# Gate products of a gated MLP read their weight sums where VectorE forms them, and ring loads and row reads take another order

## The chip, the cores and the metric

The kernel runs on one core of one Trainium2 chip. The metric is the device time of one execution, in microseconds (us). A profiled execution also leaves a trace of every instruction and every DMA.

## The reference, cut to what matters

Sigmoid attention over 8 batches, 12 heads, 448 tokens and 64 values a head, and behind it a gated MLP with a spatial product between tokens:

```python
scores = scale * np.matmul(q, k.transpose(0, 1, 3, 2)) - np.log(S)
attn = 1.0 / (1.0 + np.exp(-scores))
x = np.matmul(attn, v)            # heads side by side: (8, 448, 768)
h = np.maximum(x @ w_in, 0.0)     # (8, 448, 1024)
u, v = h[..., :512], h[..., 512:]
v_n = (v - mean(v)) / np.sqrt(var(v) + 1e-06)
v_s = np.einsum('ts,bsd->btd', w_spatial, v_n) + b_spatial[None, :, None]
out = (u * v_s) @ w_out           # (8, 448, 768)
```

## The kernel before, in words

The work goes in four rounds of two batches (`m` 0 to 3; the text counts rounds 1 to 4, so `m == BY_BLOCKS` is round 3). A round is attention, then the gate products (x with the v half of w_in, called w_g), the up products (x with w_u), the spatial products, and the output products (w_out). Every operand is split into a high and a low float32r part, and a product is three products of parts.

In rounds 3 and 4 the gate, up and output products go by blocks: each weight matrix is cut into 2 by 2 blocks, called 11, 12, 21 and 22, and seven products of block sums (a scheme of Strassen's kind, with the sums s1 to s4 in place of plain block 21 and others) take the place of eight. `by_blocks` runs over the seven, in a fixed order: ORDER_U is 11, 12, s2, s3, s1, s4, 22, ORDER_1 is 11, 12, s3, s2, s1, s4, 22. Each of the seven is two results (i = 0, 1) of nine products, so one stage is 14 slots of nine. After every slot `then(mv, i)` copies or adds the result (mv names the moving operand: 11, 21, t2, t3, t1, 22, t4). Products that share a bank of PSUM wait for the copy before them.

A block and its low part take 768 KB. A ring in SBUF (`block`, `load_block`) holds four blocks, HELD, of the seven; the rest are loaded as room comes free. The blocks lie in DRAM, where `weight_sums` put the sums: VectorE adds and subtracts, ScalarE casts the high part, VectorE forms the low part, and SP writes both out. For w_g this happens in the attention of round 3, in `spare` steps. There the plain w_g lies in SBUF too (`w_g_2`), and `keep_gate_blocks` writes its blocks to DRAM. After attention, round 3 loads the ring of w_g from DRAM again, and then that of w_u. The tags w_u, w_g and w_out are regions of SBUF used in turn by several tiles: the tile `whole`, in which attention leaves unsplit results, lies in w_out's, and `us`, the up results, in w_g's.

The gate results come with columns over partitions, but the normalization needs rows. `by_tokens` turns them: `turn` transposes quarters on VectorE and writes them to DRAM with four DMAs each (`vt` to `v`, L890), and `load` reads rows back (`rv`, L906) in four reads: a (tiles 4, 5), b (6), c (0, 1), d (2, 3). Tiles 4 to 6 need the second batch's quarters only. `steps` then takes each through `relu`, `moments` (statistics on VectorE, 1/std on GpSimd, mean subtracted on ScalarE) and `scaled` (ScalarE and VectorE), one step for each call of `spare(1)`, which `ungated` makes after every slot of the up stage. All engines run in the program's order (`in_program_order`), SP's DMA queue too: a DMA that waits holds those behind it. The tiles vt and rv share the tag tmp with three buffers.

Before, SP's order around the up stage is: the last `turn`'s writes, four blocks of w_out, the reads a and b in the second slot, then w_u's fifth block, the read c, and so on.

Of the kernel before, what the change touches and what calls it, by code (L numbers as in the profile page):

```python
# [14 lines left out]
P = 128  # L15
# [20 lines left out]
def attn_gmlp_kernel(  # L36
# [65 lines left out]
    def gate_weights(name):  # L102
        w = gate_region(name)[:, : NCC * 2 * F]
        return w.rearrange("p (k a f) -> p k a f", k=NCC, a=2)
# [378 lines left out]
    NAMES = ("11", "12", "21", "22")  # L483
    HELD = 4
# [22 lines left out]
    def gate_block(name):  # L507
        m, k = NAMES.index(name) // 2, NAMES.index(name) % 2
        return w_g[-1][:, k * KH : (k + 1) * KH, :, m * 2 * P : (m + 1) * 2 * P].bitcast(F32)

    def keep_gate_blocks():
        w7, order = KINDS["g"]
        for name in NAMES:
            if name in order:
                by = w7[order.index(name)].rearrange("p a (k c) -> p a k c", k=KH)
                for a in range(2):
                    nc.sync.dma_start(by[:, a], gate_block(name)[:, :, a])
# [7 lines left out]
    def weight_sums(stage, kind):  # L525

        w7, order = KINDS[kind]

        def whole(t):
            return t.rearrange("p (k c) -> p k c", k=KH) if kind == "g" else t  # L530

        def low(i):
            return stage[:, i, 1]

        def high(i):
            return stage[:, i, 0].bitcast(F32R)

        def add(i, a, b, op=ALU.add):
            nc.vector.tensor_tensor(whole(low(i)), a, b, op=op)

        def part(name, a):
            return gate_block(name)[:, :, a] if kind == "g" else plain(w_u[0], name, a)

        def finish(i, name):
            nc.vector.tensor_sub(low(i).bitcast(F32R), low(i), high(i).bitcast(F32))
            nc.sync.dma_start(w7[order.index(name)], stage[:, i])

        def cast(i):
            nc.scalar.copy(high(i), low(i))

        add(0, part("21", 0), part("21", 1))
        yield True
        add(0, whole(low(0)), part("22", 0))
        yield True
        add(0, whole(low(0)), part("22", 1))
        yield True
        cast(0)
        add(1, whole(low(0)), part("11", 0), ALU.subtract)
        yield True
        add(1, whole(low(1)), part("11", 1), ALU.subtract)  # L560
        yield True
        finish(0, "s1")
        yield True
        cast(1)
        add(2, part("11", 0), part("21", 0), ALU.subtract)
        yield True
        add(2, whole(low(2)), part("11", 1))
        yield True
        add(2, whole(low(2)), part("21", 1), ALU.subtract)
        yield True  # L570
        cast(2)
        add(3, part("12", 0), whole(low(1)), ALU.subtract)
        yield True
        finish(1, "s2")
        yield True
        add(3, whole(low(3)), part("12", 1))
        yield True
        cast(3)
        finish(2, "s3")
        yield True  # L580
        finish(3, "s4")
        yield True
# [108 lines left out]
    def values_by_blocks(m):  # L691
# [82 lines left out]
        turn, steps = by_tokens(m)  # L774

        def then(mv, i):
# [18 lines left out]
            elif mv == "22":  # L795
                turn(1, 0, px[i], i)
            elif mv == "t4":
                nc.vector.tensor_add(r2[:, i], py[i], r2[:, i])
                if i:
                    turn(0, 1, r2)  # L800

        def stationary(w, i, k):
            return w[:, :, (k * 2 + i) * P : (k * 2 + i + 1) * P]

        by_blocks(m, "g", stationary, x, KH, {X: px, W: pw, Y: py}, then, ORDER_1)
# [68 lines left out]
    def by_tokens(m):  # L874
# [26 lines left out]
        def load(ts):  # L901
            rv = work.tile([P, 2, 512], F32, tag="tmp", name=f"rv_{m}_{ts[0]}", bufs=3)
# [47 lines left out]
        def steps():  # L950
            a, b, c, d = (4, 5), (6,), (0, 1), (2, 3)
            yield True
            load(a)
            load(b)
            yield True
# [6 lines left out]
            load(d)  # L962
            scaled(a)
            moments(b)
            yield True
            relu(c)
            scaled(b)
# [4 lines left out]
            scaled(c)  # L972
            moments(d)
# [4 lines left out]
        return turn, steps  # L978
# [91 lines left out]
    def by_blocks(m, kind, stationary, moving, nk, ps, then, order):  # L1070
# [3 lines left out]
        for pos, name in enumerate(order):  # L1074
            mv, to = OPERANDS[name]
            if not whole:
# [19 lines left out]
            if not whole and pos + HELD < NB:  # L1096
# [4 lines left out]
    def gated_by_blocks(m):  # L1101
# [176 lines left out]
        if m >= BY_BLOCKS:  # L1278

            def ungated(mv, i):  # L1280
# [13 lines left out]
                spare(1)  # L1294

            by_blocks(m, "u", stationary, x, KH, {X: px, W: pw, Y: py}, ungated, ORDER_U)
# [374 lines left out]
    for m in range(B // 2):  # L1671
        if m == 1:
            stage = const.tile([P, 4, 2, BLOCK], F32, tag="w_out", name="w_u_sums")
            jobs.append(weight_sums(stage, "u"))
            w_g.append(gate_weights("w_g_2"))
            late[8] = [lambda: nc.sync.dma_start(w_g[-1].bitcast(F32), w_g_kept)]
        ring = []
        if m >= BY_BLOCKS:
            whole_x["tile"] = const.tile([P, 4, KH, S], F32, tag="w_out", name=f"whole_{m}")
            if m == BY_BLOCKS:  # L1680
                stage = const.tile([P, 4, 2, BLOCK], F32, tag="w_u", name="w_g_sums")
                jobs.append(weight_sums(stage, "g"))
# [9 lines left out]

            if m > BY_BLOCKS:
                late[8].append(lambda: gate_ring(range(HELD)))
# [6 lines left out]
        if m in (1, BY_BLOCKS):  # L1701
            w_u.append(const.tile([P, 2, NCC * F], F32R, tag="w_u", name=f"w_u_{m}"))
        if m == BY_BLOCKS:
            gate_ring(range(HELD))
        if m:
# [7 lines left out]
        if m >= BY_BLOCKS:  # L1713
            values_by_blocks(m)
            w_out.append(const.tile([P, 2, NFC * DM], F32R, tag="w_out", name=f"w_out_{m}"))
            for pos in range(HELD):
                load_block("out", ORDER_1, pos)
# [91 lines left out]
```

## Time and profile before

| what | value |
| --- | --- |
| time, median of 3 runs | 684.9 us (684.85 to 686.63) |
| the profiled execution, its own time | 684.99 us |
| its span, first to last instruction | 683.2 us |
| TensorE busy, share of the span | 638.3 us, 93% |
| VectorE busy | 468.1 us, 69% |
| ScalarE busy | 336.6 us, 49% |
| mean granted TensorE clock | 0.968 of full speed |

PE is TensorE's products, PEld its weight loads, DVE VectorE, ACT ScalarE, POOL GpSimd, SP the engine that issues most DMAs. A busy share is an average over stages; a stage's own limit is read from what ended its waits. L with a number is a line of the kernel before.

### The profile page before, as it was taken

To read this page: it belongs to the slowest core of one execution; us is meant where nothing else is said; L and a number is where in the kernel's file an instruction comes from. 1 tells how busy PE (TensorE), PEld (TensorE's weight loads), DVE (VectorE), ACT (ScalarE), POOL (GpSimd) and SP (SyncE) were. 2 spreads that over 40 slices of the span, in tenths; PEclk is the share of its full clock that TensorE was granted. 3 is DMA by queue.
4 is the path that set the end of the run, shared out by engine and by line. 5 is a ranking of instruction groups with operands and counts; after the bars stand their busy time and mean duration, and the time that the engine had idled before them with its cause. 6 is when DMAs were issued, how large, how long until landed. Compare 5 with 4: busy or idle time off the path is not lost.

```text
span 683.2 us, 10332 instructions
## 1 busy us (share of the span) xinstructions
PE 638.3 (93%) x4136; PEld 495.2 (72%) x4136; DVE 468.1 (69%) x645; ACT 336.6 (49%) x437; POOL 21.5 (3%) x63
## 2 busy tenths in 40 slices
PE   9999999999999999999999799359999999954997
PEld 3655889997566789998666599259975568944997
DVE  4989789897697968396986852345775558425373
ACT  6986313254788363252888520441457765035033
POOL 0000020000000020000000000100000000011000
PEclk9999999999999999999999899879999999985999
DMA  8756433499347840447394789501583385771035
GB/s 294 263 166 216 123 122 96 172 333 316 133 138 286 336 172 1 138 166 270 140 320 176 300 288 270 234 16 68 180 307 114 114 366 131 179 305 62 0 115 185
DMA packets 52815, 130.03 MB, mean 190 GB/s; under 512 B 18720, under 2 KB 27680, under 8 KB 52640
## 3 DMA queue, kind: packets, MB, share of 16 engines
q1 hardware_dynamic: 52336, 129.04, 53.9%
q8 instruction: 32, 0.52, 0.3%
q10 hardware_dynamic: 432, 0.34, 0.2%
q14 instruction: 15, 0.12, 0.0%
HBM read 95.03 MB, written 34.34 MB: 189 GB/s over the span
## 4 chain that ended last, share of the span: by engine, by line
PE 72%; DVE 14%; DMA 5%; ACT 5%; issue 2%; SPq 1%; POOL 0%; ACTq 0%; DVEq 0%
PE pav L1509 13%; PE psc L372 12%; PE o L1086 11%; PE pg L1022 7%; PE ux L1086 6%; PE pv L454 5%; PE vx L1086 5%; PE pav L421 5%; DMA rv<-v 3%; PE uy L1086 3%; PE psc L354 2%; PE vy L1086 2%; DVE wval_s L154 1%; ACT rv L910 1%; DVE stats L917 1%
## 5 line engine op out<-in xcount | busy, mean ns | idle before, releaser
L336 ACT ACTIVATE ats<-psc,bias_s 128x896 f32<-128x896 f32 x102 | 95.2, 1008 | 19.4 <-PE pav L1509 13.3
L372 PE MATMUL psc<-qks 64*128 64x448 f32 x840 | 88.7, 364 | 1.4 <-ACT at L336 1.4
L372 PEld LDWEIGHTS psc<-qks 64*128 64x128 f32 x840 | 77.2, 184 | 16.9 <-issue 6.3
L1509 PE MATMUL pav<-ats,v 64*64 64x448 f32 x720 | 76.0, 539 | 0.0
L1086 PE MATMUL ux<-x_s,w_u 128*128 128x448 f32 x162 | 44.0, 435 | 34.0 <-ACT us L1288 18.7
L1086 PEld LDWEIGHTS ux<-x_s,w_u 128*128 128x128 f32 x162 | 37.2, 234 | 40.3 <-ACT us L1288 19.7
L1022 PE MATMUL pg<-w_sp_s,mlp 128*128 128x448 f32 x320 | 65.8, 363 | 0.0
L1022 PEld LDWEIGHTS pg<-w_sp_s,mlp 128*128 128x128 f32 x320 | 59.7, 188 | 5.3 <-issue 1.2
L1509 PEld LDWEIGHTS pav<-ats,v 64*64 64x64 f32 x720 | 28.2, 132 | 37.5 <-issue 25.8
L1086 PE MATMUL o<-x_s,w_out 128*128 128x448 f32 x270 | 55.0, 362 | 0.0
L1086 PEld LDWEIGHTS o<-x_s,w_out 128*128 128x128 f32 x270 | 50.6, 188 | 3.4
L322 DVE TENSOR_TENSOR qks<-raw,qks 128x848 fp32r<-128x848 f32 x46 | 47.4, 1038 | 1.1 <-ACT qks L315 0.2
L1086 PE MATMUL vx<-x_s,w_g 128*128 128x448 f32 x144 | 32.5, 384 | 4.3 <-DMA w_g<-w_g 3.9
L1086 PEld LDWEIGHTS vx<-x_s,w_g 128*128 128x128 f32 x144 | 28.6, 201 | 8.6 <-issue 5.4
L1509 PE MATMUL pav<-at,v 64*64 64x448 f32 x216 | 32.0, 536 | 0.0
L1155 ACT CAST x_s<-g 128x896 fp32r<-128x896 f32 (+1 forms) x11 | 9.6, 876 | 39.6 <-DVE g L1152 37.5
L454 PE MATMUL pu<-x_s,w_u_s 128*128 128x448 f32 x144 | 29.0, 362 | 0.0
L454 PE MATMUL pv<-w_g_s,x_s 128*128 128x512 f32 x126 | 28.9, 390 | 0.0
L454 PE MATMUL pv<-w_g,x_s 128*128 128x512 f32 x126 | 28.9, 390 | 0.0
L454 PEld LDWEIGHTS pu<-x_s,w_u_s 128*128 128x128 f32 x144 | 27.0, 188 | 1.8
L336 ACT ACTIVATE at<-psc,bias_s 128x896 f32<-128x896 f32 x18 | 18.1, 1010 | 20.7 <-PE psc L354 14.7
L454 PEld LDWEIGHTS pv<-w_g_s,x_s 128*128 128x128 f32 x126 | 23.6, 188 | 5.6 <-PE pav L421 0.7
(234 smaller groups left out, 1057.4 us busy)
## 6 DMA issues: line engine op xcount, KB each, us to landing
raw<-qk_dram SPq DMA_DIRECT2D x47, 456.0 KB, 5.6
w_u<-w_u SPq DMA_DIRECT2D x21, 768.0 KB, 11.0
w_out<-w_out SPq DMA_DIRECT2D x21, 768.0 KB, 6.4
v<-v_dram SPq DMA_DIRECT2D x24, 448.0 KB, 4.2
w_g<-w_g SPq DMA_DIRECT2D x14, 768.0 KB, 7.3
wraw<-w_in_dram SPq DMA_DIRECT2D x12, 512.0 KB, 4.5
v<-vt SPq DMA_DIRECT2D x32, 112.0 KB, 2.5
w_g_kept<-w_g_s SPq DMA_DIRECT2D x6, 512.0 KB, 5.4
```

The source lines that it names most:

```text
L154: nc.vector.scalar_tensor_tensor(l, low, 29, l, op0=ALU.logical_shift_right, op1=ALU.bitwise_or)
L322: nc.vector.tensor_sub(s[:, 1], loaded[b, hp][:, HALF:], s[:, 0].bitcast(F32))
L336: nc.scalar.activation(at, src, AF.Sigmoid, bias=bias_s, scale=QK)
L354: nc.tensor.matmul(psc[odd * HALF : (odd + 1) * HALF, j, :S], raw[rows, :HALF], raw[rows, HALF + Q :], start=True, stop=True,)
L372: nc.tensor.matmul(psc[:, j, :S], st[rows, k : k + P], mv[rows, Q:PART], start=i == 0, stop=i == len(ops) - 1,)
L421: nc.tensor.matmul(pav[heads, odd, :S], vt[rows, t, heads], at[rows, j], start=start, stop=t == NFULL,)
L454: nc.tensor.matmul(ps, st, mv, start=i == 0, stop=i == len(ops) - 1)
L910: nc.scalar.activation(rv, rv, AF.Relu)
L1022: nc.tensor.matmul(pg[:, i, :S], st, mv, start=n == 0 and not ended, stop=n == len(ops) - 1 and ended,)
L1086: nc.tensor.matmul(out_ps, stationary(w, i, k)[:, a], moving[mv][k][c], start=(to, i) not in started and n == 0, stop=n == len(ops) - 1, s ...
L1155: nc.scalar.copy(homes[name][0][:, i], src[:, i])
L1509: ins = nc.tensor.matmul(pavs[pair][heads, i % 2, :S], vt[rows, t if t == NFULL else t + i % 2 * (NFULL + 1), heads], at[rows, j], start=i ...
```

## The change

In round 3 the gate products read plain blocks out of w_g as it lies, and the sums out of the blocks in which VectorE forms them. These are the four blocks of w_u's ring, so that the tile of w_u is made before attention, and w_u's first four blocks are loaded one by one as the gate products are through with the sums. The unsplit sums lie in the tile `whole`. In round 4 w_u's first four blocks are loaded in attention's first and second group. In rounds 3 and 4 the first four blocks of w_out are loaded from the up stage's last four sums on, not ahead of the stage; the reads a and b are issued before the last quarter is turned, b goes to `wval_s` instead of a buffer of the tag tmp, and the steps stand in another order over the slots, d's read after a's scaling. The copy of w_g for rounds 2 and 3 lies GAP elements further on in its region.

```diff
@@ -99,8 +99,8 @@
     def gate_region(name, dtype=F32R):
         return const.tile([P, NCC * 2 * F + NEAR], dtype, tag="w_g", name=name)
 
-    def gate_weights(name):
-        w = gate_region(name)[:, : NCC * 2 * F]
+    def gate_weights(name, at=0):
+        w = gate_region(name)[:, at : at + NCC * 2 * F]
         return w.rearrange("p (k a f) -> p k a f", k=NCC, a=2)
 
     w_g = [gate_weights("w_g_s")]
@@ -481,6 +481,7 @@
     ORDER_1 = ("11", "12", "s3", "s2", "s1", "s4", "22")
     ORDER_OUT = ("11", "s2", "s3", "s1", "s4", "22", "12")
     NAMES = ("11", "12", "21", "22")
+    SUMS_G = tuple(name for name in ORDER_1 if name not in NAMES)
     HELD = 4
     w7_u, w7_out, w7_g = (
         dram.tile([NB, P, 2, BLOCK], F32, name=f"w7_{n}") for n in ("u", "out", "g")
@@ -506,7 +507,7 @@
 
     def gate_block(name):
         m, k = NAMES.index(name) // 2, NAMES.index(name) % 2
-        return w_g[-1][:, k * KH : (k + 1) * KH, :, m * 2 * P : (m + 1) * 2 * P].bitcast(F32)
+        return w_g[-1][:, k * KH : (k + 1) * KH, :, m * 2 * P : (m + 1) * 2 * P]
 
     def keep_gate_blocks():
         w7, order = KINDS["g"]
@@ -514,7 +515,7 @@
             if name in order:
                 by = w7[order.index(name)].rearrange("p a (k c) -> p a k c", k=KH)
                 for a in range(2):
-                    nc.sync.dma_start(by[:, a], gate_block(name)[:, :, a])
+                    nc.sync.dma_start(by[:, a], gate_block(name)[:, :, a].bitcast(F32))
 
     def keep_plain(w7, order, w):
         for name in NAMES:
@@ -522,58 +523,55 @@
                 at = NAMES.index(name) * BLOCK
                 nc.sync.dma_start(w7[order.index(name)], w[:, :, at : at + BLOCK].bitcast(F32))
 
-    def weight_sums(stage, kind):
+    def weight_sums(kind, stage, sum_at):
 
         w7, order = KINDS[kind]
 
         def whole(t):
             return t.rearrange("p (k c) -> p k c", k=KH) if kind == "g" else t
 
-        def low(i):
-            return stage[:, i, 1]
-
         def high(i):
-            return stage[:, i, 0].bitcast(F32R)
+            return stage(i)[:, 0]
 
         def add(i, a, b, op=ALU.add):
-            nc.vector.tensor_tensor(whole(low(i)), a, b, op=op)
+            nc.vector.tensor_tensor(whole(sum_at(i)), a, b, op=op)
 
         def part(name, a):
-            return gate_block(name)[:, :, a] if kind == "g" else plain(w_u[0], name, a)
+            return gate_block(name)[:, :, a].bitcast(F32) if kind == "g" else plain(w_u[0], name, a)
 
         def finish(i, name):
-            nc.vector.tensor_sub(low(i).bitcast(F32R), low(i), high(i).bitcast(F32))
-            nc.sync.dma_start(w7[order.index(name)], stage[:, i])
+            nc.vector.tensor_sub(stage(i)[:, 1], sum_at(i), high(i).bitcast(F32))
+            nc.sync.dma_start(w7[order.index(name)], stage(i).bitcast(F32))
 
         def cast(i):
-            nc.scalar.copy(high(i), low(i))
+            nc.scalar.copy(high(i), sum_at(i))
 
         add(0, part("21", 0), part("21", 1))
         yield True
-        add(0, whole(low(0)), part("22", 0))
+        add(0, whole(sum_at(0)), part("22", 0))
         yield True
-        add(0, whole(low(0)), part("22", 1))
+        add(0, whole(sum_at(0)), part("22", 1))
         yield True
         cast(0)
-        add(1, whole(low(0)), part("11", 0), ALU.subtract)
+        add(1, whole(sum_at(0)), part("11", 0), ALU.subtract)
         yield True
-        add(1, whole(low(1)), part("11", 1), ALU.subtract)
+        add(1, whole(sum_at(1)), part("11", 1), ALU.subtract)
         yield True
         finish(0, "s1")
         yield True
         cast(1)
         add(2, part("11", 0), part("21", 0), ALU.subtract)
         yield True
-        add(2, whole(low(2)), part("11", 1))
+        add(2, whole(sum_at(2)), part("11", 1))
         yield True
-        add(2, whole(low(2)), part("21", 1), ALU.subtract)
+        add(2, whole(sum_at(2)), part("21", 1), ALU.subtract)
         yield True
         cast(2)
-        add(3, part("12", 0), whole(low(1)), ALU.subtract)
+        add(3, part("12", 0), whole(sum_at(1)), ALU.subtract)
         yield True
         finish(1, "s2")
         yield True
-        add(3, whole(low(3)), part("12", 1))
+        add(3, whole(sum_at(3)), part("12", 1))
         yield True
         cast(3)
         finish(2, "s3")
@@ -771,7 +769,7 @@
             "p (i s) -> p i s", i=2
         )
         sums["r"] = r1, r2, r3
-        turn, steps = by_tokens(m)
+        turn, first_loads, steps = by_tokens(m)
 
         def then(mv, i):
             if mv == "11":
@@ -798,11 +796,22 @@
                 nc.vector.tensor_add(r2[:, i], py[i], r2[:, i])
                 if i:
                     turn(0, 1, r2)
+                else:
+                    first_loads()
+
+        def source(name):
+            if m > BY_BLOCKS:
+                w = block("g", ORDER_1.index(name))
+            elif name in SUMS_G:
+                w = block("u", SUMS_G.index(name))
+            else:
+                return gate_block(name).rearrange("p k a c -> p a k c")
+            return w.rearrange("p a (k c) -> p a k c", k=KH)
 
         def stationary(w, i, k):
-            return w[:, :, (k * 2 + i) * P : (k * 2 + i + 1) * P]
-
-        by_blocks(m, "g", stationary, x, KH, {X: px, W: pw, Y: py}, then, ORDER_1)
+            return w[:, :, k, i * P : (i + 1) * P]
+
+        by_blocks(m, "g", stationary, x, KH, {X: px, W: pw, Y: py}, then, ORDER_1, source)
         jobs.append(steps())
 
     def gate_values(m, ts):
@@ -899,7 +908,10 @@
         state = {}
 
         def load(ts):
-            rv = work.tile([P, 2, 512], F32, tag="tmp", name=f"rv_{m}_{ts[0]}", bufs=3)
+            if len(ts) > 1:
+                rv = work.tile([P, 2, 512], F32, tag="tmp", name=f"rv_{m}_{ts[0]}", bufs=3)
+            else:
+                rv = wval_s[:, :1024].bitcast(F32).rearrange("p (i f) -> p i f", i=2)
             state[ts] = [rv]
             at = ts[0] * P
             src = rows[at : at + len(ts) * P].rearrange("(t p) f -> p t f", p=P)
@@ -947,11 +959,13 @@
                     )
                 vns[t] = vn
 
-        def steps():
-            a, b, c, d = (4, 5), (6,), (0, 1), (2, 3)
-            yield True
+        a, b, c, d = (4, 5), (6,), (0, 1), (2, 3)
+
+        def first_loads():
             load(a)
             load(b)
+
+        def steps():
             yield True
             relu(a)
             yield True
@@ -959,23 +973,26 @@
             moments(a)
             relu(b)
             yield True
-            load(d)
             scaled(a)
             moments(b)
             yield True
+            load(d)
+            scaled(b)
+            yield True
+            yield True
             relu(c)
-            scaled(b)
             yield True
             moments(c)
             relu(d)
             yield True
             scaled(c)
+            yield True
             moments(d)
             yield True
             scaled(d)
             yield True
 
-        return turn, steps
+        return turn, first_loads, steps
 
     def cols_of(b):
         return slice(0, S) if b % 2 else slice(512 - S, 512)
@@ -1067,13 +1084,15 @@
         "s1": ("t1", X), "s4": ("22", X), "22": ("t4", Y),
     }
 
-    def by_blocks(m, kind, stationary, moving, nk, ps, then, order):
+    def by_blocks(m, kind, stationary, moving, nk, ps, then, order, source=None):
 
         started = set()
         whole = kind == "out" and not m
         for pos, name in enumerate(order):
             mv, to = OPERANDS[name]
-            if not whole:
+            if source:
+                w = source(name)
+            elif not whole:
                 w = block(kind, pos)
             elif name in NAMES:
                 at = NAMES.index(name) * BLOCK
@@ -1093,7 +1112,10 @@
                     )
                 started.add((to, i))
                 then(mv, i)
-            if not whole and pos + HELD < NB:
+            if kind == "g" and m == BY_BLOCKS:
+                if name in SUMS_G:
+                    load_block("u", ORDER_U, SUMS_G.index(name))
+            elif not whole and pos + HELD < NB:
                 load_block(kind, order, pos + HELD)
 
     hid = {}
@@ -1292,7 +1314,10 @@
                 elif mv == "t4":
                     nc.vector.tensor_add(r2[:, i], py[i], r2[:, i])
                 spare(1)
-
+                if i and mv in after:
+                    load_block("out", ORDER_1, after.index(mv))
+
+            after = [OPERANDS[name][0] for name in ORDER_U[-HELD:]]
             by_blocks(m, "u", stationary, x, KH, {X: px, W: pw, Y: py}, ungated, ORDER_U)
             spare(99)
             for fcs in (lo_fc, hi_fc):
@@ -1671,15 +1696,24 @@
     for m in range(B // 2):
         if m == 1:
             stage = const.tile([P, 4, 2, BLOCK], F32, tag="w_out", name="w_u_sums")
-            jobs.append(weight_sums(stage, "u"))
-            w_g.append(gate_weights("w_g_2"))
+            jobs.append(
+                weight_sums("u", lambda i: stage[:, i].bitcast(F32R), lambda i: stage[:, i, 1])
+            )
+            w_g.append(gate_weights("w_g_2", GAP))
             late[8] = [lambda: nc.sync.dma_start(w_g[-1].bitcast(F32), w_g_kept)]
         ring = []
         if m >= BY_BLOCKS:
             whole_x["tile"] = const.tile([P, 4, KH, S], F32, tag="w_out", name=f"whole_{m}")
             if m == BY_BLOCKS:
-                stage = const.tile([P, 4, 2, BLOCK], F32, tag="w_u", name="w_g_sums")
-                jobs.append(weight_sums(stage, "g"))
+                w_u.append(const.tile([P, 2, NCC * F], F32R, tag="w_u", name=f"w_u_{m}"))
+                sum_rooms = [whole_x["tile"][:, n].rearrange("p k s -> p (k s)") for n in (0, 1, 0, 3)]
+                jobs.append(
+                    weight_sums(
+                        "g",
+                        lambda i: block("u", SUMS_G.index(f"s{i + 1}")),
+                        lambda i: sum_rooms[i][:, :BLOCK],
+                    )
+                )
                 late[4] = [keep_gate_blocks]
             late[8] = [lambda: jobs.append(wholes(m))]
 
@@ -1690,7 +1724,13 @@
                 for pos in ps:
                     load_block("g", ORDER_1, pos)
 
+            def up_ring(ps):
+                for pos in ps:
+                    load_block("u", ORDER_U, pos)
+
             if m > BY_BLOCKS:
+                late[0] = [lambda: up_ring(range(2))]
+                late[4] = [lambda: up_ring(range(2, HELD))]
                 late[8].append(lambda: gate_ring(range(HELD)))
         attention(m)
         slots_of_mlp(m)
@@ -1698,11 +1738,8 @@
         more = m < B // 2 - 1
         if m:
             spare(99)
-        if m in (1, BY_BLOCKS):
+        if m == 1:
             w_u.append(const.tile([P, 2, NCC * F], F32R, tag="w_u", name=f"w_u_{m}"))
-        if m == BY_BLOCKS:
-            gate_ring(range(HELD))
-        if m:
             for pos in range(HELD):
                 load_block("u", ORDER_U, pos)
         if m == 1:
@@ -1713,8 +1750,6 @@
         if m >= BY_BLOCKS:
             values_by_blocks(m)
             w_out.append(const.tile([P, 2, NFC * DM], F32R, tag="w_out", name=f"w_out_{m}"))
-            for pos in range(HELD):
-                load_block("out", ORDER_1, pos)
         else:
             for ts in ((0, 1), (2, 3), (4, 5), (6,)):
                 gate_values(m, ts)
```

## Rows read from the trace of the kernel before

**Rows 1.** Windows: time, then busy time by engine, granted clock, DMA share, GB/s.
```profile
381.30:412.80 31.50, 27.56 (x129) 25.59 (x127) 20.89 (x25) 9.32 (x15) 0.00 (x0) 0.89 0.90 318
412.80:460.10 47.30, 29.57 (x128) 26.18 (x127) 16.85 (x33) 17.14 (x27) 3.59 (x8) 0.82 0.48 171
...
562.60:588.80 26.20, 25.84 (x130) 23.55 (x127) 19.08 (x23) 9.33 (x15) 0.00 (x0) 1.00 0.53 135
588.80:637.00 48.20, 31.90 (x129) 27.93 (x128) 16.85 (x33) 17.14 (x27) 3.59 (x8) 0.79 0.48 167
...
385.30:388.90 3.60, 3.59 (x10) 3.21 (x11) 3.57 (x5) 0.99 (x2) 0.00 (x0) 0.50 1.02 427
...
423.60:427.40 3.80, 3.80 (x20) 3.24 (x18) 0.00 (x0) 0.00 (x0) 0.00 (x0) 1.00 1.00 411
```

**Rows 2.** Timeline of TensorE, round 3: start, duration, instructions, idle before and releaser.
```profile
385.31 9.71 PE L1086 MATMUL vx<-x_s,w_g 128*128 128x448 f32 x36 [3.94 <-DMA w_g<-w_g]
...
434.39 3.73 PE L1086 MATMUL ux<-x_s,w_u 128*128 128x448 f32 x9 [6.97 <-ACT us L1286]
...
450.97 5.76 PE L1086 MATMUL ux<-x_s,w_u 128*128 128x448 f32 x18 [10.18 <-ACT us L1288]
...
477.39 10.97 PE L1086 MATMUL o<-x_s,w_out 128*128 128x448 f32 x54
```

**Rows 3.** Timeline of TensorE, gate and up stages of round 4.
```profile
568.94 2.08 PE L1086 MATMUL vx<-x_s,w_g 128*128 128x448 f32 x9 [0.30 <-ACT vr L778]
...
588.85 3.76 PE L1086 MATMUL ux<-x_s,w_u 128*128 128x448 f32 x18
592.45 3.76 PE L1086 MATMUL uy<-x_s,w_u 128*128 128x448 f32 x18
...
610.60 3.73 PE L1086 MATMUL ux<-x_s,w_u 128*128 128x448 f32 x9 [7.18 <-ACT us L1286]
...
627.18 6.35 PE L1086 MATMUL ux<-x_s,w_u 128*128 128x448 f32 x18 [8.53 <-ACT us L1288]
```

**Rows 4.** Timeline of ScalarE in the up stage of round 3.
```profile
428.98 1.06 ACT L910 ACTIVATE rv<-rv 128x1024 f32<-128x1024 f32 x1 [11.79 <-DMA rv<-v]
...
432.07 1.33 ACT L925 ACTIVATE rv<-rv,mean 128x512 f32<-128x512 f32 x2 [2.03 <-DVE mean L923]
...
433.83 0.51 ACT L1286 COPY us<-ux 128x448 f32<-128x448 f32 x1
...
437.51 0.72 ACT L925 ACTIVATE rv<-rv,mean 128x512 f32<-128x512 f32 x1 [1.94 <-DVE mean L923]
...
444.16 1.04 ACT L910 ACTIVATE rv<-rv 128x1024 f32<-128x1024 f32 x1
...
450.40 0.51 ACT L1288 COPY us<-ux 128x448 f32<-128x448 f32 x1
```

**Rows 5.** Timeline of SP's DMA queue around the up stage of round 3.
```profile
410.25 2.43 SPq L890 DMA_DIRECT2D v<-vt  x4
...
416.89 2.33 SPq L501 DMA_DIRECT2D w_out<-w_out  x4
419.26 0.95 SPq L906 DMA_DIRECT2D rv<-v  x2
...
436.44 0.37 SPq L906 DMA_DIRECT2D rv<-v  x1
```

**Rows 6.** DMA issues, median us to landing: 405 to 440, last row 436 to 437.
```profile
rv<-v SPq DMA_DIRECT2D x3, 512.0 KB, 9.7
v<-vt SPq DMA_DIRECT2D x12, 112.0 KB, 2.5
...
rv<-v SPq DMA_DIRECT2D x1, 512.0 KB, 3.6
```

**Rows 7.** Timeline of VectorE at attention's end, rounds 3 and 4.
```profile
382.97 1.08 DVE L730 TENSOR_TENSOR whole<-pav,whole 128x896 f32<-128x896 f32 x1
...
562.74 1.09 DVE L730 TENSOR_TENSOR whole<-pav,whole 128x896 f32<-128x896 f32 x1
```

## The prediction

> **What bounds the kernel now.** I read the page first (TensorE is busy for most of the span, so only its gaps can pay), then TensorE's timeline for its idle, then the stages of rounds 3 and 4 as windows, then the timelines of ScalarE and of SP's DMA queue to see what ends those gaps. In the page's slices TensorE is at its lowest in two places, and both are the up products (the u stage) of a round that goes by blocks. Attention has no gap worth naming. The gate stage (g) of round 3 takes 31.5 us, the same 126 products in round 4 take 26.2; the u stages take 47.3 and 48.2 [rows 1]. Nine products take 1.80 us when nothing waits (592.45 − 588.85 for 18) [rows 3], so 14 such slots are 25.2 us, and the u stages lose 22.1 and 23.0 us. Slots count from T, the stage's start (412.86 in round 3, 588.85 in round 4).
>
> In g of round 3 the reader sees 3.94 us for a DMA of w_g's ring, and behind it 36 products in 9.71 us instead of 7.2 [rows 2]. In both u stages the two large idles, 6.97 and 10.18 us in round 3 [rows 2], 7.18 and 8.53 in round 4 [rows 3], end with a ScalarE copy out of a bank that the next products write. The copy is not slow: it stands in ScalarE's order behind a step on the rows of v. The first of these steps, relu(a), starts at 428.98, 16.1 us after T, after 11.79 us of waiting for rv's DMA, and from there to the copy at 450.40 ScalarE and VectorE hand the rows to and fro without a pause [rows 4]. That read is late because SP issued it at 419.26, directly behind four w_out blocks of 768 KB issued from 416.89, which nobody needs before 477.39 [rows 2, 5]; it took 9.7 us to land, where a later read of the same size with nothing ahead took 3.6 [rows 6]. So what ends last in u is the row chain, and it starts late.
>
> **The change, part by part.**
>
> *w_g as it lies and its sums in place.* Removes seven ring loads of round 3 and the 3.94 us wait. Its products then start with the end of attention, as in round 4 (26.2). But VectorE is later here: the first full sum of the last pair (L730) starts at 382.97, 1.6 us after attention's end at 381.4, in round 4 0.1 us after 562.6 [rows 7], and ScalarE's copies, which already cost round 4 0.30 us [rows 3], stand behind it. So 26.2 + 1.5 = 27.7: gain 3.8 us, bounds 3.0 (a further 0.8) to 5.3 (as round 4). The sums keep their VectorE and ScalarE instructions, with other addresses: nothing. That products read w_g in a longer stride I take at nothing, since 128 columns still lie together; a loss is bounded in the rivals.
>
> *The ring loads of w_u.* Round 3: each is issued when a sum's block is free, the first four blocks of 3.6 us before T; a block of 768 KB takes 1.9 us at 411 GB/s [rows 1], so they land in time. Round 4: they move from the end of attention, behind w_g's, into attention's first two groups, behind loads of q and k, where SP next waits for TensorE anyway; nothing, at worst 3.8 us twice (two blocks ahead of a needed load).
>
> *w_out's loads and the first reads.* In SP's order the reads a and b now stand ahead of the last four transposed writes, and the w_out blocks behind the read d. For read a: the four writes before it are issued from 410.25 to 412.68, T − 0.2 [rows 5], and land 2.5 us after issue [rows 6], at T + 2; issue 0.5 and landing 3.6 [rows 6] give relu(a) at A = T + 5 to 6. In round 3 w_u blocks stand on both sides of those writes; 1.9 us of their 3.8 lie in the way, less what overlaps: A = T + 6.5. In round 4 there are none, but VectorE's first statistic stands behind its sum for the third slot (ends near T + 6.2, and it comes 1.1 us after relu(a) starts), which acts like A = T + 5.1. Read b needs no third buffer now (it goes to wval_s, last read in attention), and read d waits for scaled(a), as before.
>
> *The new order of steps.* What TensorE meets is the copy of the first t1 sum, which the products of "22" wait for at T + 18.0 (ten slots). Ahead of it on ScalarE, from relu(a): to the end of b's mean, 428.98 to 438.23, less the 0.41 of a copy that moves, 8.84; two copies and the scaling of b, 0.41 + 0.72 + 0.41 = 1.54; relu(c) and moments(c), as a's from 428.98 to 433.40, 4.42; relu(d) 1.04 [rows 4]; the copy until its products run, 450.40 to 450.97, 0.57 [rows 2, 4]. Sum 16.4, so the stage loses D = A + 16.4 − 18.0 = A − 1.6. That is 4.9 us in round 3 and 3.5 in round 4, nearly all in one idle before "22". An idle of 3.94 us was followed by half clock (9.71 for 7.2, and 0.50 granted) [rows 1, 2], one of 0.30 was not (2.08 for nine) [rows 3]. 3.5 is nearer 3.94, so I take a fall in both rounds at 2.2 us each, between 9.71 − 7.2 = 2.5 and 3.73 − 1.80 = 1.9 [rows 2]; bounds 0 and 2.5. Scaled(d) ends within T + 25 + D, when the spatial products begin with other tiles: nothing. Read c is needed at A + 10.4 and can be issued from T + 7.5, after the last writes land; read d at A + 14.8, and its buffer is free at A + 7.5 (436.44 against 428.98) [rows 4, 5]: both in time. Block "22" of w_u stands behind d on SP, issued near T + 13, needed at T + 21.6 + D; with 3.6 us as for a read: in time. The w_out blocks follow it; the first is needed 17 us after the stage's end.
>
> Sum: 3.8 + (22.1 − 4.9 − 2.2) + (23.0 − 3.5 − 2.2) = 3.8 + 15.0 + 17.3 = 36.1 us. The profiled execution took 684.99 us, of which 683.20 are span; the median of the runs is 684.9. 685.0 − 36.1 = 648.9.
>
> **The rivals.**
>
> *The reads land late all the same.* If writes and w_u's blocks in the queue keep relu(a) until T + 10 to 13 (the 9.7 us landing [rows 6] in place of 3.6 gives T + 12), D is 8.4 to 11.4, and the sum 3.8 + 45.1 − 4.4 − 2D = 27.7 to 21.7: 657 to 663. For it: a read waits for DRAM writes whose landing was covered by w_out's issue before, so its price is seen nowhere. Against: the writes' own 2.5 us [rows 6], and 3 MB less ahead of the read. The Trainium skill speaks for it (DMA: Bandwidth & Descriptors, "Anatomy of one DMA — SWDGE (gpsimd) path"): the semaphore comes only once the last byte is confirmed in its target, DRAM being the heaviest. Its fixed cost is some 2 us, with which the row of 2.5 agrees. Chance 0.17.
>
> *All goes well.* A at the floor in both rounds and no fall of the clock: 3.8 + 18.6 + 19.5 = 41.9, so 643. Against it: the idle of 3.5 us left. Chance 0.13.
>
> *Slower.* SP takes its queue in order, and now reads that wait stand ahead of writes and of w_u's blocks 5 to 7. If they hold SP, relu(a) and the blocks are late together, and TensorE pays 1 us for each. It decides from 2(A − 1.6) = 45.1 + 3.8, A = T + 26, 10 us later than now. Nothing in the rows holds a read so long. Slower 0.03, and 0.03 for stopping near there, at no change.
>
> **How the numbers follow.** Forecast 0.64, its own range 645 to 655: upward A two us later in both rounds (+4) and the smaller gain in g, downward one clock fall less and g as in round 4 (−2.2, −1.5). I say 649. The range 642 to 660 leaves out the two ends at or above the old time (0.06), the late half of the first rival (0.07) and some of the second (0.02). A difference of 0.3% is about what a measurement of this kernel can tell from none. Faster 0.94, same 0.03, slower 0.03.
>
> **What would show it.** The g stage of round 3 without a DMA wait, 27 to 28 us. On SP, the reads directly behind "22"'s four writes and w_out after the read d. Relu(a) at T + 5 to 7 instead of 16. One idle of 3 to 5 us before "22" and little before t1; u stages of 30 to 33 us. No new idle in attention. I am wrong if relu(a) comes after T + 8, if the chain from it to the t1 copy isn't near 16 us, or if attention of rounds 3 and 4 grows.

## The result, and the profile after

The changed kernel takes 651.4 us (median of 4 runs, 649.57 to 653.22), the kernel before 685.24 beside it: a ratio of 0.9503, 95% interval 0.9466 to 0.9539. The forecast was 649 in 642 to 660. The profiled execution took 649.57 us with a span of 647.2, against 684.99 and 683.2. It is the fastest of the four (649.57, 649.99, 652.82 and 653.22), so what is read from its trace, 36.0 us of span, is 2 us more than the 33.8 between the medians.

The windows of the two gate and up stages after, with the columns of [rows 1]:

```profile
382.00:409.80 27.80, 25.90 (x131) 23.59 (x128) 20.72 (x25) 9.33 (x15) 0.00 (x0) 1.00 0.42 102
409.80:442.50 32.70, 27.60 (x127) 24.73 (x126) 14.31 (x30) 15.54 (x25) 3.60 (x8) 0.95 0.87 298
545.50:571.70 26.20, 25.84 (x130) 23.55 (x127) 19.06 (x23) 9.33 (x15) 0.00 (x0) 1.00 0.53 134
571.70:600.90 29.20, 25.83 (x128) 23.53 (x128) 14.37 (x30) 15.59 (x25) 3.59 (x8) 1.00 0.79 276
```

Against [rows 1] the gate stage of round 3 went from 31.5 to 27.8 us, the up stages from 47.3 and 48.2 to 32.7 and 29.2. Of the 37.3 us that these three stages gave, 27.6 are idle of TensorE. The other 9.7 are busy time: it fell from 27.56, 29.57 and 31.90 us to 25.90, 27.60 and 25.83 for about the same products, as the granted clock of the stages rose from 0.89, 0.82 and 0.79 to 1.00, 0.95 and 1.00. TensorE's timeline after shows what idle is left, round 3 first, round 4 last:

```profile
387.50 2.08 PE L1105 MATMUL vx<-x_s,w_g 128*128 128x448 f32 x9 [1.60 <-ACT vr L776]
...
428.46 5.46 PE L1105 MATMUL ux<-x_s,w_u 128*128 128x448 f32 x18 [3.65 <-ACT us L1308]
435.20 3.88 PE L1105 MATMUL ux<-x_s,w_u 128*128 128x448 f32 x18 [1.27 <-ACT us L1310]
...
586.81 3.87 PE L1105 MATMUL ux<-x_s,w_u 128*128 128x448 f32 x18 [0.51 <-ACT us L1308]
593.55 3.88 PE L1105 MATMUL ux<-x_s,w_u 128*128 128x448 f32 x18 [2.86 <-ACT us L1310]
```

The DMA wait of 3.94 us is gone, a wait of 1.60 for ScalarE's copies stands in its place, and idles of 6.97 to 10.18 [rows 2, 3] became 0.51 to 3.65. L1308 copies the t2 sums, for which the t1 products wait, and L1310 the t1 sums, for which the products of "22" wait. ScalarE's timeline tells why, with T now 409.80 and 571.74:

```profile
419.15 1.06 ACT L922 ACTIVATE rv<-rv 128x1024 f32<-128x1024 f32 x1 [5.03 <-DMA rv<-v]
...
433.69 1.04 ACT L922 ACTIVATE rv<-rv 128x1024 f32<-128x1024 f32 x1
434.64 0.51 ACT L1310 COPY us<-ux 128x448 f32<-128x448 f32 x1
...
577.50 1.06 ACT L922 ACTIVATE rv<-rv 128x1024 f32<-128x1024 f32 x1 [1.43 <-DMA rv<-v]
```

Relu(a) starts at T + 9.35 in round 3 and T + 5.76 in round 4, before at T + 16.1 [rows 4]. From there to the copy of the first t1 sum it is 15.5 us (434.64 − 419.15) instead of 21.4. SP's queue in round 3 has the reads ahead of the last quarter's writes, and w_out last:

```profile
407.76 2.46 SPq L899 DMA_DIRECT2D v<-vt  x4
410.31 1.65 SPq L502 DMA_DIRECT2D w_u<-w_u  x1
414.96 0.38 SPq L918 DMA_DIRECT2D rv<-v  x1
...
415.94 2.26 SPq L899 DMA_DIRECT2D v<-vt  x4
...
427.13 2.13 SPq L502 DMA_DIRECT2D w_out<-w_out  x4
```

Stage by stage, from TensorE's timelines of the two profiled executions (start of a stage to start of the next, differences taken before rounding):

| stage | before | after | gain | forecast |
| --- | --- | --- | --- | --- |
| gate products, round 2 | 28.7 | 29.5 | −0.8 | 0 |
| gate, round 3 | 31.5 | 27.8 | 3.7 | 3.8 |
| up, round 3 | 47.3 | 32.7 | 14.6 | 15.0 |
| attention, round 4 | 59.9 | 60.5 | −0.5 | 0 |
| up, round 4 | 48.1 | 29.1 | 19.0 | 17.3 |
| sum | | | 36.0 | 36.1 |

The sum is the difference of the spans, 683.2 − 647.2. Two rows were not foreseen; round 2's shows in the page's groups (busy, mean ns of one), before and after:

```profile
L454 PE MATMUL pv<-w_g,x_s 128*128 128x512 f32 x126 | 28.9, 390 | 0.0
```

```profile
L454 PE MATMUL pv<-w_g,x_s 128*128 128x512 f32 x126 | 29.7, 396 | 0.0
```

### The profile page after: what moved, and what is told of

It reads as the page before. It is cut to its first block, busy times and chain, and to the rows that moved or that the text cites. A ratio compares the mean times of both kernels' runs of the same rounds, so it can differ in the third digit from the quotient of the medians.

```text
span 647.2 us, 10315 instructions
## 1 busy us (share of the span) xinstructions
PE 629.9 (97%) x4136; PEld 487.4 (75%) x4136; DVE 467.6 (72%) x645; ACT 336.1 (52%) x437; POOL 21.5 (3%) x63
## 4 chain that ended last, share of the span: by engine, by line
PE 71%; DVE 16%; ACT 5%; DMA 3%; issue 2%; SPq 1%; POOL 0%; ACTq 0%; DVEq 0%
PE pav L1534 14%; PE psc L372 14%; PE o L1105 12%; PE pg L1039 8%; PE pv L454 6%; PE pav L421 5%; PE ux L1105 3%; PE vx L1105 3%; PE uy L1105 3%; PE psc L354 2%; DMA rv<-v 1%; DMA v<-vt 1%; DVE wval_s L154 1%; PE vy L1105 1%; SPq L899 1%
## 5 line engine op out<-in xcount | busy, mean ns | idle before, releaser
L1105 PE MATMUL ux<-x_s,w_u 128*128 128x448 f32 x162 | 35.7, 376 | 8.3 <-ACT us L1308 4.2
L1105 PEld LDWEIGHTS ux<-x_s,w_u 128*128 128x128 f32 x162 | 31.4, 196 | 12.0 <-ACT us L1308 4.9
L454 PEld LDWEIGHTS pv<-w_g,x_s 128*128 128x128 f32 x126 | 23.6, 188 | 6.3 <-issue 0.7
L421 PE MATMUL pav<-ats,v 128*64 128x448 f32 (+1 forms) x144 | 27.1, 544 | 0.0
```

Source lines behind the costliest of these rows:

```text
L421: nc.tensor.matmul(pav[heads, odd, :S], vt[rows, t, heads], at[rows, j], start=start, stop=t == NFULL,)
L454: nc.tensor.matmul(ps, st, mv, start=i == 0, stop=i == len(ops) - 1)
L1105: nc.tensor.matmul(out_ps, stationary(w, i, k)[:, a], moving[mv][k][c], start=(to, i) not in started and n == 0, stop=n == len(ops) - 1, s ...
```

## The experiments

The theory: the up stage's loss is the time from T to relu(a), A, plus a chain on ScalarE fixed by the order of the steps, less the slots that TensorE has until it needs the copy. Rivals: that only the reads' arrival counts, that w_out's place in the queue is the whole cause, or that fewer ring loads free the queue by themselves.

**e1_place0: the copy of w_g back at the start of its region.**

```diff
-            w_g.append(gate_weights("w_g_2", GAP))
+            w_g.append(gate_weights("w_g_2"))
```

> The changed kernel with the copy of w_g for rounds 2 and 3 back at the start of its region instead of GAP elements on. Theory (the place costs): round 2's 126 gate products take 28.7 us again instead of 29.5, all else stays, some 0.8 us less than the changed kernel's 651.4. Rival (something else, such as traffic, made them slower): they stay at 29.5 us.

Measured: 650.85 us, ratio 0.9492 (0.9469 to 0.9515). TensorE's timeline, round 2 and round 4:

```profile
226.16 28.86 PE L454 MATMUL pv<-w_g,x_s 128*128 128x512 f32 x126
...
593.88 5.47 PE L1105 MATMUL ux<-x_s,w_u 128*128 128x448 f32 x18 [2.86 <-ACT us L1310]
```

The 126 products are back at 28.86, so the place made them slower, not traffic. Of the total little can be said: the same idle of 2.86 us that left 18 products at 3.88 in the changed kernel's profile is followed by 5.47 here, a fall of the clock that takes 1.6 us, more than the 0.8 that the place gives.

**e2_gate_only: the first part of the change alone.** `load`, `steps` and w_out's loads as in the kernel before.

```diff
         def first_loads():
-            load(a)
-            load(b)
+            pass
...
             w_out.append(const.tile([P, 2, NFC * DM], F32R, tag="w_out", name=f"w_out_{m}"))
+            for pos in range(HELD):
+                load_block("out", ORDER_1, pos)
```

> The changed kernel with w_out's loads, the reads of rows and the steps as before, so that only w_g as it lies, the sums in place and the new loads of w_u's ring are left. Theory (the up stages hang on reads and steps alone): the gate stage of round 3 takes 27.8 us, the up stages stay at 47 to 48; 682 to 684 us. Rival (fewer ring loads also bring the rows early): relu(a) near T + 10 and an up stage near 40 us in round 3; near 675.

Measured: 685.47 us, ratio 0.9996 (0.9982 to 1.0009): no gain, where 1 to 3 us were expected. The gate stage does take 27.8 us, but in ScalarE's timeline, and then TensorE's, of round 3:

```profile
428.73 1.06 ACT L919 ACTIVATE rv<-rv 128x1024 f32<-128x1024 f32 x1 [14.04 <-DMA rv<-v]
```

```profile
434.14 3.73 PE L1102 MATMUL ux<-x_s,w_u 128*128 128x448 f32 x9 [9.22 <-ACT us L1305]
...
450.72 6.62 PE L1102 MATMUL ux<-x_s,w_u 128*128 128x448 f32 x18 [8.54 <-ACT us L1307]
```

and on SP, behind w_out's four blocks:

```profile
418.39 1.05 SPq L915 DMA_DIRECT2D rv<-v  x2
```

T came 2.5 us earlier than before (410.36), relu(a) at the same moment, 428.73 against 428.98 [rows 4], now T + 18.4, and the up stage took 50.4 us. The read was issued at 418.39, 0.9 us sooner than before [rows 5], and relu(a) starts 10.3 us after that. What the gate stage won, the up stage gave back in waiting for a read whose time the end of the gate stage does not set.

**e3_wout_back: w_out's first four blocks ahead of the up stage again, all else as changed.**

```diff
             w_out.append(const.tile([P, 2, NFC * DM], F32R, tag="w_out", name=f"w_out_{m}"))
+            for pos in range(HELD):
+                load_block("out", ORDER_1, pos)
...
-                if i and mv in after:
-                    load_block("out", ORDER_1, after.index(mv))
```

> The changed kernel with w_out's first four blocks loaded ahead of the up stage again; the reads a and b stay ahead of them. Theory (only the reads' place in the queue counts, not where w_out is): relu(a) stays at T + 9.3 and T + 5.8; w_u's fifth block now lands behind w_out, so t1 may start at T + 18 to 19 in round 4 too; up stages of 33 and 30 to 31 us, 651 to 654. Rival (w_out ahead of the stage is itself the delay): up stages back to 38 us or more, over 662.

Measured: 658.45 us, ratio 0.9616 (0.9591 to 0.9642), between theory and rival. SP's, ScalarE's and TensorE's timelines of round 3:

```profile
418.37 3.30 SPq L502 DMA_DIRECT2D w_out<-w_out  x4
421.77 0.39 SPq L502 DMA_DIRECT2D w_u<-w_u  x1
422.27 0.42 SPq L918 DMA_DIRECT2D rv<-v  x1
```

```profile
419.07 1.06 ACT L922 ACTIVATE rv<-rv 128x1024 f32<-128x1024 f32 x1 [4.67 <-DMA rv<-v]
...
433.97 1.06 ACT L922 ACTIVATE rv<-rv 128x1024 f32<-128x1024 f32 x1 [4.60 <-DMA rv<-v]
```

```profile
432.64 5.58 PE L1105 MATMUL ux<-x_s,w_u 128*128 128x448 f32 x18 [7.91 <-DMA w_u<-w_u]
```

Relu(a) stays at T + 9.0 (T = 410.07), and at T + 5.8 in round 4, as the theory has it. But w_u's fifth block and the read c lie behind w_out's 3 MB: TensorE waits 7.91 us for the one, relu(c) 4.60 for the other. The stages take 37.1 and 33.9 us. I had put the fifth block some 4 us too early in round 3 (its products start at T + 22.6) and had taken c's read as harmless. So w_out's place counts, though for other loads than those whose lateness it caused before.

**e4_old_steps: the order of steps from before.** Reads a and b early, w_out late.

```diff
+            yield True
             relu(a)
             yield True
             load(c)
             moments(a)
             relu(b)
             yield True
+            load(d)
             scaled(a)
             moments(b)
             yield True
-            load(d)
-            scaled(b)
-            yield True
-            yield True
             relu(c)
+            scaled(b)
             yield True
             moments(c)
             relu(d)
             yield True
             scaled(c)
-            yield True
             moments(d)
```

> The changed kernel with the steps on the rows in the order and slots of before; reads a and b early, w_out late. Theory (the chain from relu(a) to the copy of the first t1 sum sets the stage, and the old order makes it 22 us long instead of 16.4): the stages lose 13 and 10 us, up stages of 38 and 35 us and a fall of the clock, some 664. Rival (only the rows' arrival counts): up stages as in the changed kernel, under 654.

Measured: 666.66 us, ratio 0.9722 (0.9702 to 0.9741); stages of 41.0 and 38.0 us. ScalarE's and TensorE's timelines of round 3:

```profile
420.05 1.06 ACT L922 ACTIVATE rv<-rv 128x1024 f32<-128x1024 f32 x1 [5.62 <-DMA v<-vt]
...
441.50 0.51 ACT L1308 COPY us<-ux 128x448 f32<-128x448 f32 x1
```

```profile
429.79 2.08 PE L1103 MATMUL ux<-x_s,w_u 128*128 128x448 f32 x9 [2.23 <-ACT us L1306]
...
442.06 5.62 PE L1103 MATMUL ux<-x_s,w_u 128*128 128x448 f32 x18 [10.18 <-ACT us L1308]
```

From relu(a) to the copy 21.45 us, as in the kernel before, and the idle of 10.18 before "22" is back to the hundredth [rows 2] though the rows came 6 us sooner. What the earlier rows took away is most of the idle before t1, 6.97 then and 2.23 at the most here. The stages are 3 us longer than the 38 and 35 that I had put beside one fall of the clock; the fall makes 2 of these in round 3 (18 products in 5.62 us, not 3.6), and round 4 has one too. With the reads early, the order of the steps is worth some 15 us of the 34. The new order with the reads late was not run, so what it gives by itself is not known.

**e5_wout_late: the kernel before, with w_out's loads moved alone.**

```diff
-            for pos in range(HELD):
-                load_block("out", ORDER_1, pos)
...
+                if i and mv in after:
+                    load_block("out", ORDER_1, after.index(mv))
```

> The kernel before with one part of the change alone: w_out's first four blocks loaded from the up stage's last four sums on. Reads and steps as before. Theory (w_out ahead of the reads is what makes relu(a) late, and the old steps then keep a chain of 22 us): relu(a) at T + 8 to 10 instead of 16, the stages lose some 13 to 15 us instead of 22 to 23, 668 to 672. Rival (in run e3_wout_back relu(a) did not move with w_out, so w_out's place matters for c and the ring alone): relu(a) stays past T + 13, over 678.

Measured: 671.31 us, ratio 0.9786 (0.9762 to 0.9811). SP's and ScalarE's timelines of round 3 (T = 413.36):

```profile
417.46 1.07 SPq L906 DMA_DIRECT2D rv<-v  x2
```

```profile
422.54 1.06 ACT L910 ACTIVATE rv<-rv 128x1024 f32<-128x1024 f32 x1 [4.85 <-DMA rv<-v]
...
443.98 0.51 ACT L1288 COPY us<-ux 128x448 f32<-128x448 f32 x1
```

Relu(a) at T + 9.2, and 21.4 us from it to the copy: stages of 40.8 and 41.2 us. So w_out ahead of the reads was what made them late in the kernel before, and taking it away is worth 14 to 15 us with the old steps.

**e6_first_late: the reads a and b in the up stage's first slot.**

```diff
         def first_loads():
-            load(a)
-            load(b)
+            pass
...
         def steps():
+            load(a)
+            load(b)
             yield True
             relu(a)
```

> The changed kernel with the reads a and b issued in the up stage's first slot, behind the writes of the last quarter, and not ahead of them. Theory (in round 3 these reads wait for the writes ahead of them anyway, in round 4 they lose the time of four issues and a landing): relu(a) near T + 9.5 in round 3 and T + 8 to 9 in round 4, up stages near 33 and 32, 653 to 655. Rival (the early issue is most of the gain): up stages over 36, over 658.

Measured: 653.72 us, ratio 0.953 (0.9516 to 0.9544). ScalarE's timeline, rounds 3 and 4 (T = 410.06 and 573.08):

```profile
420.26 1.06 ACT L922 ACTIVATE rv<-rv 128x1024 f32<-128x1024 f32 x1 [5.87 <-DMA rv<-v]
...
582.17 1.06 ACT L922 ACTIVATE rv<-rv 128x1024 f32<-128x1024 f32 x1 [4.76 <-DMA rv<-v]
```

T + 10.2 and T + 9.1, 0.9 and 3.3 us later than as changed; stages of 33.6 and 32.5. Issuing these two reads before the last quarter is turned is worth 4.2 us between the profiled stages, and 2.3 between the medians. The clock of these stages is no steady price: after an idle of the same 3.65 us, 18 products took 3.88 us in round 3 and 5.46 in round 4 of this one execution.

```profile
429.57 3.88 PE L1106 MATMUL ux<-x_s,w_u 128*128 128x448 f32 x18 [3.65 <-ACT us L1309]
...
591.48 5.46 PE L1106 MATMUL ux<-x_s,w_u 128*128 128x448 f32 x18 [3.65 <-ACT us L1309]
```

**e7_ring_behind: w_u's third and fourth block of round 3 behind the reads a and b.**

```diff
                 else:
                     first_loads()
+                    if m == BY_BLOCKS:
+                        for pos in (2, 3):
+                            load_block("u", ORDER_U, pos)
...
-                if name in SUMS_G:
+                if name in SUMS_G[:2]:
```

> The changed kernel with w_u's third and fourth block of round 3 loaded behind the reads a and b, not among the writes of the turned rows. Theory (these blocks stretch the writes' landing to 4.2 us and hold relu(a) of round 3 at T + 9.3): relu(a) at T + 6 to 7, its up stage 29 to 30 us instead of 32.7, some 648.5. Rival (the writes' own small packets set their landing): relu(a) stays past T + 8.5 and the blocks now come late for their products, 652 or more.

Measured: 648.11 us, ratio 0.9452 (0.9437 to 0.9468). ScalarE's, then TensorE's timeline of rounds 3 and 4 (T = 409.91):

```profile
415.07 1.06 ACT L925 ACTIVATE rv<-rv 128x1024 f32<-128x1024 f32 x1 [0.83 <-DMA rv<-v]
```

```profile
419.89 5.43 PE L1108 MATMUL ux<-xs,w_u 128*128 128x448 f32 x18 [2.61 <-DMA w_u<-w_u]
...
433.21 3.87 PE L1108 MATMUL ux<-x_s,w_u 128*128 128x448 f32 x18 [0.69 <-ACT us L1313]
...
591.11 5.45 PE L1108 MATMUL ux<-x_s,w_u 128*128 128x448 f32 x18 [2.85 <-ACT us L1313]
```

Relu(a) starts at T + 5.2, so the two blocks were what held it in round 3. The rival's half came too: the third block lands late for s2, 2.61 us of wait. The stage takes 30.6 us.

**e9_steps: a third order of steps.** The mean's subtraction (`centered`) is a step of its own.

```diff
             moments(a)
             relu(b)
+            centered(a)
             yield True
-            scaled(a)
             moments(b)
-            yield True
+            scaled(a)
             load(d)
+            yield True
+            centered(b)
             scaled(b)
             yield True
             yield True
-            relu(c)
             yield True
-            moments(c)
-            relu(d)
             yield True
-            scaled(c)
+            relu(c)
+            moments(c)
             yield True
+            relu(d)
             moments(d)
+            centered(c)
+            scaled(c)
+            centered(d)
             yield True
             scaled(d)
```

> The changed kernel with the steps in a third order: all copies of the t2 sums ahead of anything of reads c and d, c's and d's steps behind the copies of the t1 sums, and the mean subtracted in a step of its own. Nothing else moves. Theory (what is left of the stage's loss is the copies' place in ScalarE's order, D = A - 1.6): the copy of the first t1 sum no longer waits, losses of 2 us and 0 to 1 us, up stages of 27 and 26 us, some 642 to 643. Rival (the rows' chain ends last whatever the order, so the spatial products wait in place of the up products): at most 2 us less, over 648.

Measured: 642.09 us, ratio 0.9359 (0.9345 to 0.9373). TensorE's timeline, round 3 and round 4, and SP's of round 3:

```profile
425.12 3.94 PE L1112 MATMUL ux<-x_s,w_u 128*128 128x448 f32 x18 [0.46 <-ACT us L1315]
431.31 5.43 PE L1112 MATMUL ux<-x_s,w_u 128*128 128x448 f32 x18 [2.25 <-DMA w_u<-w_u]
...
582.96 7.36 PE L1112 MATMUL ux<-x_s,w_u 128*128 128x448 f32 x36
```

```profile
421.73 4.16 SPq L918 DMA_DIRECT2D rv<-v  x2
425.99 0.89 SPq L502 DMA_DIRECT2D w_u<-w_u  x2
```

The time is the theory's, the stages are not: I had put them at 27 and 26 us. Round 4's up stage takes 25.2 us: 14 slots of 1.80 and not one idle. Round 3's takes 30.7, of which 2.25 is a wait for a block of w_u that stands on SP behind the read d, which I had moved ahead of it, and half clock after that.

**e10_all: what the runs point to, together.**

```diff
                 started.add((to, i))
+                if i and kind == "g" and m == BY_BLOCKS and name == "s1":
+                    load_block("u", ORDER_U, 2)
                 then(mv, i)
...
                     first_loads()
+                    if m == BY_BLOCKS:
+                        load_block("u", ORDER_U, 3)
...
             scaled(a)
-            load(d)
             yield True
+            load(d)
             centered(b)
```

These edits stand on e9_steps (its `load(d)` one slot later), with e1's place of w_g and e7's `SUMS_G[:2]`.

> All that the runs point to, together: the third order of steps, with the read d one slot later so that w_u's sixth block stands ahead of it on SP; w_u's third block of round 3 issued ahead of the second quarter's writes and its fourth behind the reads a and b; the copy of w_g at the start of its region. Theory: round 2's gate products 28.7 us, relu(a) of round 3 at T + 5 to 6, up stages of 25.2 to 26 us in both rounds, some 5.8 us under the run e9_steps, so 636 to 637. Rival (w_u's blocks have only changed places, and another of them is late for its products): round 3's up stage stays over 28 us, 639 or more.

Measured: 636.52 us (median of 5, 636.23 to 637.79), ratio 0.9287 (0.9274 to 0.93), so some 15 us under the changed kernel. ScalarE's and TensorE's timelines of round 3 (T = 408.65), the last row round 4:

```profile
414.31 1.06 ACT L924 ACTIVATE rv<-rv 128x1024 f32<-128x1024 f32 x1 [1.32 <-DMA rv<-v]
```

```profile
423.06 7.53 PE L1114 MATMUL ux<-x_s,w_u 128*128 128x448 f32 x36
430.43 3.76 PE L1114 MATMUL uy<-x,w_u 128*128 128x448 f32 x18
434.03 4.17 PE L1048 MATMUL pg<-w_sp_s,mlp 128*128 128x448 f32 x20
...
577.33 7.36 PE L1114 MATMUL ux<-x_s,w_u 128*128 128x448 f32 x36
```

Both up stages are at their floor, 25.4 and 25.2 us.

## Why the prediction was right, point by point

- **What bounds.** Right: the row chain ended last in the up stages and started late behind w_out (e5: relu(a) from T + 16.1 to T + 9.2 by that move alone).
- **D = A − 1.6.** Right. With the A measured it gives 7.8 and 4.2 us; the stages lost 7.5 and 3.9. With the old steps the same chain is 21.4 us long (e4), with a third order it holds TensorE up by 0.46 us in one round (e9) and then not at all (e10).
- **A.** The likeliest was T + 6.5 and an effective 5.1; round 4 had 5.76, round 3 had 9.35. That is one of the two terms of the sum that were mis-sized (the clock, below, is the other): I let the turned rows' writes land 2.5 us after issue, as before [rows 6], and added for w_u's blocks 1.9 us less what overlaps. In the DMA issues after, of the writes around them (405 to 411 us) and of the read (414.5 to 416):

```profile
v<-vt SPq DMA_DIRECT2D x8, 112.0 KB, 4.0
...
rv<-v SPq DMA_DIRECT2D x1, 512.0 KB, 4.1
```

  With these blocks among them the writes take 4.0 us, SP holds read a until 414.96, T + 5.2 and not T + 2, and the read itself takes 4.1 instead of 3.6. e7 took both away: relu(a) at T + 5.2. The first rival, late reads, was thus half true in round 3 and by its own mechanism, and one of my own signs of being wrong, relu(a) after T + 8, was met there. The idles fell elsewhere than I had said for the same reason: in round 3 the larger one, 3.65 us, stands before t1, since the copies of the t2 sums also stand behind steps on the rows, and only in round 4 does it stand before "22" (2.86).
  The Trainium skill's rule that was weighed there (DMA: Bandwidth & Descriptors, "Anatomy of one DMA — SWDGE (gpsimd) path"), that a write's semaphore waits for its confirmation, some 2 us of fixed cost, agrees with the 2.5 us of writes that have no load among them [rows 6], though the section describes GpSimd's path and these writes go out on SP. The further 1.5 us, to 4.0, come with the loads between: in e7, without them, the writes take 2.5 again.
- **The clock.** Two falls at 2.2 us each were taken; the profile shows one, after the 3.65 us in round 3:

```profile
428.40:431.00 2.60, 2.54 (x7) 2.28 (x8) 1.30 (x2) 2.01 (x4) 0.00 (x0) 0.51 1.04 414
```

  It added nothing there: the copy that the next products needed started at 434.64 only, by the chain. So 4.4 us were taken off for falls that cost nothing in this execution; they cover what A cost in round 3 and the 1.3 us lost in round 2 and in attention. That the sum, 36.1, meets the 36.0 of the trace is luck: its errors cancel, and in the fastest execution. Between the medians the change gave 33.8.
- **The gate stage.** 3.7 against 3.8. But it isn't a term by itself: alone it gave 0 (e2), since the reads' landing set the end of the up stage. It counts only once the reads are early.
- **Costed at nothing.** The ring loads of w_u in round 4's attention: no new idle in its groups. Its 0.5 us, another of my signs of being wrong if a small one, stand at the first scores: from their start to the first products behind the wait for ScalarE's sigmoid it is 4.88 us instead of 4.33, of which the wait is 0.78 instead of 0.59. Over the runs that wait went from 0.29 to 1.19. The same stretch takes 4.72 us in e5, which loads w_u as before, and 4.03 in e9, which loads it as changed, so these loads are not shown to be the cause; what is stays open. The other address of w_g was not free: 0.8 us in round 2 (e1).
- **w_out's move.** Counted as part of A only. e3 shows a second use: without it the read c and w_u's fifth block are late, 7 us in all.

## What to carry to other kernels

Where a chain over two engines runs beside TensorE, ask which of its steps stand ahead of a copy that TensorE needs, in program order: moving copies ahead of steps took round 4's stage to its floor (e9), and round 3's once the loads stood in due order too (e10), with the same 645 instructions on VectorE and 437 on ScalarE. An in-order DMA queue is a schedule: order it by due time and look at each load behind a wait, for an early load that waits can hold a block that is due sooner (e9), and a late bulk load moved back can save another load than the one it used to delay (e3). A gain in one stage is real only if the next stage's input doesn't come at a fixed time (e2).

## What the runs showed of the hardware that was not expected

An idle of TensorE of the same length is or isn't followed by half clock: after 2.86 us 18 products took 3.88 us in the changed kernel's round 4 and 5.47 in e1's, and e6 shows both after 3.65 us in one execution. Executions of the changed kernel lie 3.6 us apart, those of e10_all, which has no such idle, 1.6. That the falls make this spread is argued, not shown, and those of e7, which has idles of 2.61 and 2.85 us, lie 0.8 apart. Moving w_g, the operand that streams through TensorE in 126 products of round 2, by GAP (48 elements) in SBUF changed their mean from 390 to 396 ns at a granted clock of 1.00; why was not tried.
